# Attention output of three batches transposed by DMA instead of TensorE, with the early weight loads, the warm-up and the instruction order changed along with it

## The chip, the cores and the metric

The kernel runs on one core of a Trainium2 chip. The metric is the device time of one execution in microseconds (us). The kernel before had been measured at 306.03 us, the median of three runs from 305.15 to 315.46 us; the verdicts "faster", "same" and "slower" are set at 2%.

Engines are named as in the profile: PE is TensorE, PEld its weight loads, DVE is VectorE, ACT is ScalarE, POOL is GpSimd, and SP is SyncE, which issues most DMAs here. PSUM is the memory that matmuls write their results to. "First HP" is the first matmul of the feed-forward part, and "HP to end" is the time from its start to the end of the last matmul.

## The reference, cut to what matters

There are 4 batches with 8 heads, 768 positions and head dimension 64. Each query chooses, by a bound on its scores, 6 of 24 chunks of 32 keys, and attends causally to those. The attention output, 3072 tokens of 512 values, goes through two matrix products with a hard-swish between.

```python
ub  = sum(maximum(q * k_min, q * k_max))          # per query and chunk of 32 keys
top = argsort(where(causal, ub, -1e9))[..., -6:]
attn = softmax(where(in_top_chunk & causal, q @ k.T / 8, -1e9))
x = (attn @ v).transpose(0, 2, 1, 3).reshape(3072, 512)
h = x @ w_in                                      # w_in 512 x 2048
out = (h * clip(h + 3, 0, 6) / 6) @ w_out         # w_out 2048 x 512
```

## The kernel before

The program is planned in Python. Each operation is given to a planner with its engine, its dependencies and the ring buffers that it takes; a string `SEQUENCE` of priorities decides the order in which the planner emits ready operations. The 32 head-and-batch combinations go in 16 pairs of heads, four pairs for each batch. For a pair, K and Q are loaded and transposed on PE (tiles KT, QT), bounds and chunk choice are made (UBP, SEL, SLT), scores go to SPS, ACT takes the exponential into PT, POOL applies the causal mask, and PE multiplies by V (PVP). DVE's norm writes the attention output Xb, tokens on the partitions. The feed-forward part needs it with features on the partitions (XT). It works in eight groups of 384 tokens, two for a batch.

The attention of the next batches is interleaved with the feed-forward part of earlier ones, so that PE always has something to do. In code and in profile lines, `...` stands for what is left out.

```python
WARMUP = (10, 9)
...
    def castv():          # pair i's V, to bf16 on POOL; its operation is st[i]["o_v"]
...
    WGATE = (0, 0, 0, 4, 4, 0, 8, 3)   # weight load n is issued after the V cast of pair WGATE[n]
    ...
            iss = add("POOL", 0.63, f"w{n}",
                      lambda c=c: nc.gpsimd.dma_start(WIN[:, :, c:c + DFF // 4], wi[:, :, c:c + DFF // 4]),
                      deps=[st[WGATE[n]]["o_v"]], chain="wi")        # chain: w0, w1, ... in this order
...
        def do_xt():
            for k0 in range(0, KT_HID, 2):
                def tr(k0=k0, ps=ps):                      # 6 transposes of 128x128 on PE
                    T = new(ps, [P, 2, GRP], BF16, "XTP")
                    for kk in range(2):
                        for t in range(TPG):
                            nc.tensor.transpose(T[:, kk, t * P:(t + 1) * P],
                                                xb[b].obj[:, blk0 + t, (k0 + kk) * P:(k0 + kk + 1) * P], IDENTB[:])
                def ev(k0=k0, ps=ps):                      # and their copy out of PSUM on DVE
                    nc.vector.tensor_copy(xt.obj[:, k0:k0 + 2, :], ps.obj[:])
...
                        nc.tensor.matmul(T[:, f, 0:GRP], lhsT=WIN[:, kt, (f0 + f) * P:(f0 + f + 1) * P],
                                         rhs=xt.obj[:, kt, :], start=(kt == 0), stop=(kt == KT_HID - 1))   # HP
...
            for _ in range(WARMUP[n]):                     # before the first K, and after the first Q
                nc.tensor.transpose(T[:], IDENT32[:], IDENT32[:])
```

The softmax here doesn't subtract the row's maximum and nothing guards it: scores larger than these inputs give would overflow.

Of the kernel before, what the change touches and what calls it, by code (L numbers as in the profile page):

```python
# [15 lines left out]
P = 128  # L16
# [113 lines left out]
WARMUP = (10, 9)  # L130
# [4 lines left out]
Q10 H6.10 q15 O4.1.0 P10.0 L0 H7.4 H7.12 P10.1 U4 P5.1 R1 S10.1 V5 K0 S8.1 H7.6 R0 H3.8 H3.6 X4.2 H7.10 V10  # L135
O3.0.4 S9.0 L13 S0.3 q0 U0 P12.1 O2.1.0 H1.10 O6.0.8 U10 v0 S4.4 O6.1.8 H7.14 X1.0 X7.2 O2.0.4 K2 P4.1 K4 S11.1
L4 v12 O3.2.0 S0.1 O7.0.8 C1 W0 C7 K10 X3.2 v2 L5 k6 q2 Q2 v13 O3.0.12 v9 Q15 O2.0.8 C5 V2 O5.1.0 P6.0 P9.1
H5.12 O6.1.12 L12 O0.1.0 k1 H2.6 S5.1 v15 S0.5 H3.0 w5 Q1 H6.14 q14 B3 S0.0 O1.2.12 H1.2 U9 H7.0 k15 V4 L11 S0.4
H0.6 Q11 K6 H2.12 O1.0.4 v10 U2 O0.0.12 X7.0 C13 v3 Q14 S11.4 q10 P1.1 P9.0 O6.1.4 O3.1.8 S3.3 U3 K9 O3.1.4 B4
O4.0.12 H4.0 H6.0 S14.2 Q3 S7.0 H2.4 S7.2 O1.2.8 H1.12 K13 H1.14 B1 k2 X3.0 S10.4 K8 O6.0.12 H2.10 S13.1 w0 S9.1  # L140
H3.4 H4.4 H0.12 U1 R10 O3.2.8 O7.1.12 S3.1 P7.1 O6.0.0 S2.2 V9 O2.2.0 K3 B7 U15 P8.1 Q5 S2.1 R3 O4.0.0 H7.2
O1.0.12 H2.14 S6.1 P2.1 O4.0.4 H0.10 H0.0 X4.0 S5.0 H2.2 O5.2.0 S8.5 w7 S14.5 v8 U7 S12.0 S2.4 R5 P8.0 O2.1.12
O6.2.4 k0 k14 O1.0.8 S2.5 B9 S10.3 k10 O4.2.8 S9.3 k13 X1.2 H0.2 O7.1.8 S11.5 k3 O4.1.8 O5.0.0 P13.1 v11 O7.0.4
S3.0 H0.14 C15 O3.0.0 K15 k8 S6.2 O0.2.0 q1 R8 k9 S8.3 R11 V1 L14 q12 L2 O2.0.12 H7.8 S7.1 H0.4 U6 S10.2 O5.1.12
O0.0.0 S14.1 V13 k4 H1.8 L7 H4.10 S6.3 H3.10 O6.1.0 S4.3 w6 S9.2 S14.0 k7 H3.14 O3.1.0 q7 S7.5 S5.4 v4 H6.6
O4.2.12 K11 O4.1.4 S6.5 P1.0 S11.0 H6.12 O1.1.8 O1.2.0 H5.0 B8 O0.1.12 S6.4 K5 P3.1 H6.4 B2 k5 H4.8 H3.2 S4.2
# [19 lines left out]
def kernel(  # L166
# [541 lines left out]
```

## Time and profile before

| what | before | where it is read |
|---|---|---|
| span of the profiled run | 304.2 us | page |
| PE busy | 290.5 us (95%) | engine table of the page |
| first HP starts | 63.55 us | the trace |
| HP to end | 237.1 us | the trace |
| the 96 XTP transposes, start to start in the stream | 0.064 us each | the trace: 72 of them take 4.6 us |

The engine table of the page of the kernel before gives busy time, share of the span and instructions of each engine.

```profile
PE 290.5 (95%) x3027; PEld 182.0 (60%) x3027; DVE 168.8 (55%) x460; ACT 178.6 (59%) x219; POOL 92.0 (30%) x168
```

An average over the whole span hides that there are two stages. The windows view cuts the span; its columns are the window, its length, then the busy time and instruction count of each engine, the granted PE clock as a share of its full speed, the DMA share and GB/s.

```profile
0.00:20.00 20.00, 14.57 (x120) 11.57 (x122) 12.21 (x39) 6.15 (x9) 15.07 (x25) 0.95 1.23 200
20.00:40.00 20.00, 16.64 (x277) 11.65 (x275) 14.11 (x61) 15.11 (x18) 11.28 (x21) 0.96 1.15 209
40.00:63.55 23.55, 22.80 (x418) 16.76 (x413) 17.83 (x71) 22.02 (x27) 16.70 (x32) 1.00 1.04 197
63.55:300.80 237.25, 236.51 (x2224) 142.03 (x2221) 124.69 (x292) 134.94 (x167) 48.97 (x90) 1.00 0.30 71
```

After the first HP PE is busy 236.5 of 237.25 us, so only less PE work seems to help there. Before it, PE is idle for 9.5 us. The waits view of PE says for what (total, times, longest):

```profile
PE KT L319 <- DMA KS<-in_k_dram: 2.9, 2, 2.1
PE SLT L436 <- DVE SEL_130 L419: 2.5, 1, 2.5
PE WRM L650 <- POOL IDENT_114 masks.py:199: 1.4, 1, 1.4
PE QT L319 <- DMA QS<-in_q_dram: 1.4, 2, 0.7
```

These are loads of K and Q and one chunk choice on DVE. The DMA engines are busy all through this stage (the last two columns of the windows), and three weight loads of 512 KB each are issued in it.

### The profile page before, as it was taken

The numbers are of one execution on the slowest core, as the hardware profiler recorded it, in microseconds if no ns is written. First come the engines' busy times: TensorE is split into PE (matmuls) and PEld (weight loads), VectorE is DVE, ScalarE is ACT, GpSimd is POOL, SyncE is SP. The second block draws the span as 40 slices with busy tenths as digits, with TensorE's granted clock in tenths as the row PEclk, the third lists the DMA queues.
The fourth block names the chain that finished last, engine by engine and source line by source line (L and its number), as shares of the span: only waits on it lengthen the run. The fifth ranks groups of instructions, "written<-read, shape, count | busy, mean of one in ns | idle before, by whom it ended". The sixth has DMA issues, their size and how long they took to land.

```text
span 304.2 us, 7326 instructions
## 1 busy us (share of the span) xinstructions
PE 290.5 (95%) x3027; PEld 182.0 (60%) x3027; DVE 168.8 (55%) x460; ACT 178.6 (59%) x219; POOL 92.0 (30%) x168
## 2 busy tenths in 40 slices
PE   6977899999999999999999999999999999999995
PEld 5845567766666566756555556666656765545444
DVE  4587887756769965672444165967413575505300
ACT  1547689987466258876644555496737654624311
POOL 8576566844105235612000242450303100000000
PEclk9979999999999999999999999999999999999999
DMA  9999999995807989620200131100010000011012
GB/s 171 218 214 199 214 214 219 168 197 119 139 1 171 245 184 241 134 54 34 54 36 36 37 110 48 37 2 1 2 71 36 2 2 0 0 72 69 34 70 71
DMA packets 83122, 29.84 MB, mean 98 GB/s; under 512 B 75792, under 2 KB 80144, under 8 KB 83088
## 3 DMA queue, kind: packets, MB, share of 16 engines
q1 hardware_dynamic: 77296, 24.78, 37.1%
q0 software_dynamic: 4224, 4.19, 8.6%
q10 hardware_dynamic: 1568, 0.39, 0.7%
q8 instruction: 24, 0.39, 0.6%
q14 instruction: 10, 0.08, 0.1%
HBM read 27.26 MB, written 6.29 MB: 110 GB/s over the span
## 4 chain that ended last, share of the span: by engine, by line
PE 84%; DMA 6%; DVE 4%; ACT 2%; issue 1%; POOL 1%; SPq 1%; ACTq 0%; DVEq 0%; POOLq 0%
PE HP L564 27%; PE OP L590 26%; PE PVP L507 7%; DMA QS<-in_q_dram 6%; PE SPS L466 6%; PE SPS L471 4%; PE UBP L386 3%; PE QT L319 3%; PE KT L319 2%; PE XTP L544 2%; PE UBQ L408 2%; PE OP L611 1%; ACT PT L477 1%; DVE KM L337 1%; PE SLT L436 1%
## 5 line engine op out<-in xcount | busy, mean ns | idle before, releaser
L477 ACT ACTIVATE PT<-SPS 128x1024 bf16<-128x1024 f32 (+1 forms) x96 | 82.2, 924 | 18.1 <-PE SPS L471 15.7
L574 DVE SCALAR_TENSOR_TENSOR GT<-U,HP 128x768 bf16<-128x768 bf16 x64 | 60.7, 953 | 51.1 <-ACT U L568 36.2
L564 PE MATMUL HP<-XT,WIN 128*128 128x384 bf16 x512 | 86.8, 326 | 0.0
L590 PE MATMUL OP<-WOUT,GT 128*128 128x512 bf16 x368 | 84.1, 380 | 0.0
L568 ACT ACTIVATE U<-HP,THREE 128x768 bf16<-128x768 f32 x64 | 57.7, 901 | 39.2 <-PE HP L564 39.1
L564 PEld LDWEIGHTS <-WIN 128*128 128x128 bf16 x512 | 49.3, 98 | 32.7
L481 POOL TENSOR_SCALAR_AFFINE_SELECT PT<-PT 128x256 bf16<-128x256 bf16 x96 | 38.6, 407 | 82.0 <-ACT PT L477 81.6
L590 PEld LDWEIGHTS <-GT 128*128 128x128 bf16 x368 | 35.0, 98 | 40.2 <-issue 1.5
L596 ACT ACTIVATE OT<-OP 128x512 f32<-128x512 f32 x23 | 13.8, 598 | 42.4 <-PE OP L590 34.9
L466 PE MATMUL SPS<-RHS,LHS 64*128 64x512 bf16 (+3 forms) x256 | 34.1, 312 | 0.7 <-ACT PT L477 0.6
L471 PE MATMUL SPS<-SELT,EM 64*128 64x288 bf16 (+6 forms) x384 | 32.5, 250 | 0.0
L512 DVE RECIPROCAL RINV<-PVP 128x6 f32<-128x6 f32 x32 | 6.0, 191 | 37.7 <-PE PVP L507 37.6
L507 PEld LDWEIGHTS <-PT 128*128 128x128 bf16 x672 | 23.2, 97 | 4.1 <-issue 1.6
L471 PEld LDWEIGHTS <-EM 64*128 64x128 bf16 x384 | 18.6, 95 | 7.6 <-issue 0.5
L352 POOL CAST LHS<-KTS 128x768 bf16<-128x768 f32 x15 | 12.4, 827 | 32.8 <-ACT KTS L333 30.0
L466 PEld LDWEIGHTS <-LHS 64*128 64x128 bf16 x256 | 11.3, 95 | 11.3 <-issue 7.5
L517 DVE TENSOR_TENSOR Xb<-PVP,RINV 128x384 bf16<-128x384 f32 x32 | 17.4, 553 | 0.8
L373 POOL CAST RHS<-QTS 128x768 bf16<-128x768 f32 x16 | 15.2, 958 | 8.5 <-ACT QTS L363 8.5
L333 ACT COPY KTS<-KT 128x768 f32<-128x768 f32 x15 | 11.9, 800 | 9.5 <-PE KT L319 8.3
L319 PE MATMUL KT<-IDENT_114,KS 128*128 128x128 f32 x96 | 14.2, 292 | 2.9 <-DMA KS<-in_k_dram 2.9
L363 ACT COPY QTS<-QT 128x768 f32<-128x768 f32 x16 | 12.5, 810 | 4.2 <-PE QT L319 3.9
L319 PEld LDWEIGHTS KT<-IDENT_114,KS 128*128 128x128 f32 x96 | 11.8, 151 | 4.6 <-ACT PT L477 2.3
(113 smaller groups left out, 249.8 us busy)
## 6 DMA issues: line engine op xcount, KB each, us to landing
VS<-in_v_dram SPq DMA_DIRECT2D x32, 192.0 KB, 4.5
KS<-in_k_dram SPq DMA_DIRECT2D x31, 192.0 KB, 4.3
QS<-in_q_dram SPq DMA_DIRECT2D x31, 192.0 KB, 4.9
out_dram<-OT SPq DMA_DIRECT2D x23, 256.0 KB, 2.0
WIN<-in_moe_w_in_dram POOLq DMA_DIRECT2D x4, 512.0 KB, 9.2
WOUT<-in_moe_w_out_dram POOLq DMA_DIRECT2D x4, 512.0 KB, 9.4
out_dram<-OT SPq DMA_DIRECT2D x2, 128.0 KB, 1.7
KS<-in_k_dram ACTq DMA_DIRECT2D x1, 192.0 KB, 3.8
```

The source lines that it names most:

```text
L319: nc.tensor.transpose(T[:, j * P:(j + 1) * P], src.obj[:, j].rearrange("p e d -> p (e d)"), IDENT32[:])
L373: nc.gpsimd.tensor_copy(new(s["rhs"], [P, S], BF16, "RHS")[:], qts.obj[:])
L466: nc.tensor.matmul(T[:, e, c:c + hi - lo], lhsT=s["lhs"].obj[e * D:(e + 1) * D, j * P:(j + 1) * P], rhs=s["rhs"].obj[e * D:(e + 1) * D, lo ...
L471: nc.tensor.matmul(T[:, e, c:c + hi - lo], lhsT=EM[e * D:(e + 1) * D, h, j * P:(j + 1) * P], rhs=s["selt"].obj[e * D:(e + 1) * D, x:x + hi ...
L477: nc.scalar.activation(T[:, :, 0:w], sp.obj[:, :, 0:w], ACT.Exp, scale=scale)
L481: nc.gpsimd.affine_select(out=dv, in_=dv, pattern=[[0, 2], [1, P]], compare_op=A.is_ge, fill=0.0, base=0, channel_multiplier=-1)
L507: nc.tensor.matmul(T[:, qb, :], lhsT=t[:, e, c:c + P], rhs=fx(s["vb"])[:, e, j, :], start=(j == 0), stop=(j == qb))
L517: nc.vector.tensor_tensor(out=xb[b].obj[:, :, h * D:(h + 1) * D], in0=pv.obj[:, :, 0:D], in1=s[("ri", e)][:].to_broadcast([P, NBLK, D]), o ...
L564: nc.tensor.matmul(T[:, f, 0:GRP], lhsT=WIN[:, kt, (f0 + f) * P:(f0 + f + 1) * P], rhs=xt.obj[:, kt, :], start=(kt == 0), stop=(kt == KT_H ...
L568: nc.scalar.activation(new(u, [P, 2, GRP], BF16, "U")[:], hp.obj[:, :, 0:GRP], ACT.Relu, bias=THREE[:], scale=1.0)
L574: nc.vector.scalar_tensor_tensor(out=gt.obj[:, f0:f0 + 2, :], in0=u.obj[:], scalar=6.0, in1=hp.obj[:, :, 0:GRP], op0=A.min, op1=A.mult)
L590: nc.tensor.matmul(T[:, :], lhsT=gt.obj[:, f, t * P:(t + 1) * P], rhs=WOUT[:, f, :], start=(f == 0), stop=(f == FT - 1))
```

## The change

The intent has three parts. For batches 1 to 3 the DMA engines transpose Xb into XT, which takes 72 of 96 transposes from PE. Two of the three early weight loads go behind the third V cast, out of the way of the K and Q loads. The warm-up of PE's clock uses real fp32 matmuls instead of transposes. A new `SEQUENCE` (order) was found for it.

```diff
-WARMUP = (10, 9)
+WARMUP = ((6, 0.43), (8, 0.21), (3, 0.21))
...   (SEQUENCE replaced as a whole)
-    plan = Plan(rings, dict(PE=2.0, DVE=3.2, ACT=2.2, POOL=9.3, LD=0.3, ST=0.0), place)
+    plan = Plan(rings, dict(PE=1.4, DVE=3.2, ACT=2.2, POOL=9.3, LD=0.3, ST=0.0), place)
-    WGATE = (0, 0, 0, 4, 4, 0, 8, 3)
+    WGATE = (0, 2, 1, 5, 6, 5, 6, 2)
...
+            if b >= XDMA:                                   # XDMA = 1
+                for t in range(TPG):                        # TPG = 3 blocks of 128 tokens
+                    def tr(t=t):
+                        if t == 0:
+                            new(xt, [P, TPG, KT_HID, P], BF16, "XT")
+                        nc.sync.dma_start_transpose(xt.obj[:, t], xb[b].obj[:, blk0 + t, :])
+                    ops.append(add("LD", 0.7, f"X{g}.{t}", tr, deps=norms[b] + ops[:1], take=[xt] if t == 0 else [],
+                                   use=[xb[b]] if t == 0 else [xb[b], xt]))
+                return ops
...   (batch 0: as before, into the new layout of XT)
-                                         rhs=xt.obj[:, kt, :], start=(kt == 0), stop=(kt == KT_HID - 1))
+                                         rhs=xt.obj[:, :, kt, :], start=(kt == 0), stop=(kt == KT_HID - 1))
...
-            for _ in range(WARMUP[n]):
-                nc.tensor.transpose(T[:], IDENT32[:], IDENT32[:])
+            for _ in range(WARMUP[n][0]):
+                nc.tensor.matmul(T[:], lhsT=IDENT32[:], rhs=IDENT32[:], start=True, stop=True)
...
+            if i == 0 and f is plan_K:
+                plan_warm(2, st[0]['o_ktr'])                # three more, between the first K and the first Q
```

More of the change, by code (lines that the diff above doesn't have):

```diff
@@ L127, in run @@
         return order
-WARMUP = (10, 9)
+WARMUP = ((6, 0.43), (8, 0.21), (3, 0.21))
 SEQUENCE = """
-Q10 H6.10 q15 O4.1.0 P10.0 L0 H7.4 H7.12 P10.1 U4 P5.1 R1 S10.1 V5 K0 S8.1 H7.6 R0 H3.8 H3.6 X4.2 H7.10 V10
-O3.0.4 S9.0 L13 S0.3 q0 U0 P12.1 O2.1.0 H1.10 O6.0.8 U10 v0 S4.4 O6.1.8 H7.14 X1.0 X7.2 O2.0.4 K2 P4.1 K4 S11.1
-L4 v12 O3.2.0 S0.1 O7.0.8 C1 W0 C7 K10 X3.2 v2 L5 k6 q2 Q2 v13 O3.0.12 v9 Q15 O2.0.8 C5 V2 O5.1.0 P6.0 P9.1
-H5.12 O6.1.12 L12 O0.1.0 k1 H2.6 S5.1 v15 S0.5 H3.0 w5 Q1 H6.14 q14 B3 S0.0 O1.2.12 H1.2 U9 H7.0 k15 V4 L11 S0.4
@@ L139 @@
-H0.6 Q11 K6 H2.12 O1.0.4 v10 U2 O0.0.12 X7.0 C13 v3 Q14 S11.4 q10 P1.1 P9.0 O6.1.4 O3.1.8 S3.3 U3 K9 O3.1.4 B4
-O4.0.12 H4.0 H6.0 S14.2 Q3 S7.0 H2.4 S7.2 O1.2.8 H1.12 K13 H1.14 B1 k2 X3.0 S10.4 K8 O6.0.12 H2.10 S13.1 w0 S9.1
-H3.4 H4.4 H0.12 U1 R10 O3.2.8 O7.1.12 S3.1 P7.1 O6.0.0 S2.2 V9 O2.2.0 K3 B7 U15 P8.1 Q5 S2.1 R3 O4.0.0 H7.2
-O1.0.12 H2.14 S6.1 P2.1 O4.0.4 H0.10 H0.0 X4.0 S5.0 H2.2 O5.2.0 S8.5 w7 S14.5 v8 U7 S12.0 S2.4 R5 P8.0 O2.1.12
-O6.2.4 k0 k14 O1.0.8 S2.5 B9 S10.3 k10 O4.2.8 S9.3 k13 X1.2 H0.2 O7.1.8 S11.5 k3 O4.1.8 O5.0.0 P13.1 v11 O7.0.4
@@ L144 @@
-S3.0 H0.14 C15 O3.0.0 K15 k8 S6.2 O0.2.0 q1 R8 k9 S8.3 R11 V1 L14 q12 L2 O2.0.12 H7.8 S7.1 H0.4 U6 S10.2 O5.1.12
-O0.0.0 S14.1 V13 k4 H1.8 L7 H4.10 S6.3 H3.10 O6.1.0 S4.3 w6 S9.2 S14.0 k7 H3.14 O3.1.0 q7 S7.5 S5.4 v4 H6.6
-O4.2.12 K11 O4.1.4 S6.5 P1.0 S11.0 H6.12 O1.1.8 O1.2.0 H5.0 B8 O0.1.12 S6.4 K5 P3.1 H6.4 B2 k5 H4.8 H3.2 S4.2
-q13 O0.1.4 B13 V3 O1.1.12 v6 Q12 Q8 H4.6 C8 B12 H1.6 H6.2 B6 S4.1 O3.2.12 v7 P11.0 S4.5 B10 O4.1.12 S7.4 O0.0.4
-H1.4 P0.1 S8.4 O2.1.8 P15.1 H4.12 X2.2 S2.0 S7.3 k11 w4 O7.0.12 S1.4 B11 H5.14 L3 S8.0 w1 U5 H3.12 q5 V15 v14
@@ L149 @@
-C14 O2.2.12 v5 B14 S4.0 S12.1 S8.2 C2 S13.0 X5.2 S3.5 S12.3 P14.0 R12 S1.3 O4.2.4 O2.1.4 O5.0.8 O0.1.8 S9.5 S3.2
-B15 S5.3 q6 C9 R4 S6.0 O5.0.4 O7.2.0 P2.0 S1.1 P11.1 S5.5 S15.5 X2.0 q9 S14.3 C0 V7 P6.1 H2.0 O2.0.0 q8 L1 H4.2
-q4 H0.8 Q6 O7.1.4 H4.14 S9.4 K1 L15 O3.0.8 q11 U13 S3.4 O2.2.8 O4.0.8 V12 S13.2 S5.2 H5.2 S15.3 P7.0 U11 O7.2.12
-P13.0 V14 C6 H2.8 P0.0 S10.5 U12 w3 P4.0 U14 O3.1.12 H1.0 H5.10 S11.3 R7 V8 q3 S12.2 Q4 V11 O1.2.4 W1 R2 O5.1.4
-H6.8 O0.2.8 O5.1.8 P14.1 C11 L9 C10 S15.1 S15.4 O7.1.0 O6.2.12 K7 C3 V0 S10.0 S0.2 O6.2.0 C12 L6 v1 C4 K12 w2
@@ L154 @@
-K14 B5 S13.5 S12.5 O7.2.8 H5.6 O0.0.8 O2.2.4 P12.0 R9 O4.2.0 S13.3 O6.2.8 O5.2.4 X5.0 Q13 L8 V6 O0.2.12 O6.0.4
-R15 O3.2.4 U8 P5.0 O0.2.4 X0.0 R14 S15.2 S14.4 L10 Q7 P15.0 X6.2 O5.2.12 S12.4 B0 S13.4 O5.0.12 S1.5 Q9 R13 X6.0
-O5.2.8 Q0 S1.2 S11.2 O7.0.0 O1.1.0 k12 H5.4 H5.8 S15.0 R6 S2.3 S1.0 P3.0 X0.2 O1.1.4 O1.0.0
+H6.10 H7.14 Q10 H7.12 H7.4 P5.1 H3.6 P10.1 q15 P12.1 K9 S8.1 O6.1.8 v12 X7.2 O3.0.12 v0 H3.8 H6.14 q10 X3.2
+S10.1 S11.1 K4 O3.0.4 R0 U4 L13 P10.0 U10 S9.0 P4.1 S6.4 S0.3 q14 L11 H6.0 Q15 O6.1.4 P9.1 Q5 O6.1.12 q0 v2
@@ new lines @@
+O3.2.0 S0.0 q2 P9.0 k10 H2.12 Q11 S5.1 V5 H7.0 S7.0 L0 X1.0 H2.14 V9 P8.0 K8 k14 H7.10 v9 H3.0 X2.1 H0.10 H3.4
+v10 K0 q1 U3 S4.4 S13.1 R8 X3.1 R5 C7 H2.4 O1.2.12 C1 S0.5 S6.3 H2.10 O2.0.4 v13 K13 k1 K10 H6.12 B1 O6.0.12 R1
+O4.1.0 O6.0.8 P6.0 H3.10 H1.14 X6.1 O7.0.8 O6.2.4 w5 H7.6 S12.0 V4 O6.0.0 O1.0.12 H0.14 O3.2.8 V10 B7 k9 Q14
+O2.1.0 O4.2.8 H2.6 S9.3 R10 S8.5 P8.1 H0.6 S0.1 S2.1 L5 U0 H1.10 B3 S12.1 O1.0.8 K6 V2 U15 O3.1.4 C0 H1.12 K11
+L4 P11.0 S0.4 S9.1 H0.0 k15 H4.0 O4.0.0 U2 Q2 P13.1 H0.2 w0 V12 H1.2 B4 U9 O0.0.12 H0.4 v3 O5.1.0 W0 S8.2 S10.2
@@ new lines @@
+Q8 X4.2 H0.12 H6.6 B9 O5.0.0 B15 k6 S2.2 L12 R3 P1.1 w6 X4.1 O1.1.12 O5.2.0 S7.2 k3 H6.4 W2 O4.0.12 q12 O4.1.12
+q13 X3.0 S8.3 H3.12 L2 S11.4 v11 Q3 V1 S10.4 U5 O3.1.8 S14.5 O1.0.4 S6.2 L14 q7 C5 O7.1.12 k8 U8 k11 O4.1.8
+O3.1.12 S14.0 O2.0.12 q8 S3.3 S6.0 Q12 Q1 S2.4 C13 P13.0 P7.0 S9.4 K1 H6.2 O1.2.4 v8 O1.1.8 V15 P15.1 O1.2.0 R12
+H5.12 O5.1.12 H7.2 S5.0 v15 O2.0.8 O0.1.4 H2.2 X2.2 X1.2 X7.0 O7.1.8 k0 H2.0 R11 S11.0 S7.1 O7.2.12 B5 w7 H3.14
+S1.3 S8.4 H7.8 X7.1 S14.3 S4.3 H4.8 S4.1 O4.0.4 S2.5 U6 B8 X5.2 S15.5 O2.2.0 k13 v6 S5.3 S7.5 q6 S8.0 S9.2 K15
@@ new lines @@
+v4 H1.8 H5.2 k2 q4 P0.1 U7 S5.4 v5 P7.1 O4.2.12 S6.5 v7 O3.1.0 O0.1.0 q5 P3.1 O1.2.8 O5.0.8 H0.8 S4.5 S7.4 S1.4
+L7 V3 S3.1 O3.0.8 S1.1 V7 O0.1.12 S7.3 k7 B13 H5.10 S2.0 S3.0 P1.0 S11.5 U13 P11.1 O6.2.8 W1 V8 O4.2.4 P4.0 V13
+S4.0 V11 O7.0.4 Q6 H2.8 B10 C15 k5 S13.0 X2.0 O0.0.0 U1 O2.2.8 U12 P6.1 O3.2.12 L8 L6 U14 O6.2.12 P14.0 S10.3 Q4
+S5.5 S9.5 P2.0 K2 C8 w4 w3 O6.1.0 X6.2 V6 S14.1 O0.1.8 k4 S14.2 S10.0 R13 S6.1 U11 B12 P2.1 S5.2 O4.1.4 O3.0.0
+S13.2 O2.1.8 P12.0 X5.1 C14 K12 O2.2.12 O2.1.12 L15 H1.6 H6.8 H3.2 L1 H5.0 K3 H4.4 V0 q11 H4.6 O2.1.4 v14 C6 L9
@@ new lines @@
+H4.10 O7.1.4 B6 S15.3 H4.2 C3 O6.2.0 S4.2 O7.2.0 H1.0 C10 O0.2.0 O7.1.0 X4.0 S0.2 C11 C2 B2 S11.3 O5.1.4 O4.0.8
+w1 H5.14 S13.5 O6.0.4 P5.0 S10.5 S15.1 P14.1 O7.2.8 L3 K14 P0.0 H4.12 O5.1.8 R7 S12.4 S3.5 O2.0.0 S12.5 S12.3 R4
+O0.0.4 K5 C9 S11.2 C12 O7.0.12 O4.2.0 S15.4 Q13 R9 R2 S12.2 O0.2.12 V14 O1.1.0 O3.2.4 S1.2 q3 X6.0 H4.14 R14 L10
+B14 S3.2 R15 S3.4 B0 H1.4 X5.0 R6 q9 C4 Q0 S14.4 B11 w2 X0.0 v1 k12 H5.8 S1.5 H5.6 O1.1.4 O0.0.8 K7 P15.0 O0.2.4
+O5.0.4 O5.2.4 S15.2 O5.2.8 S13.3 O1.0.0 S13.4 O0.2.8 S1.0 S15.0 O5.2.12 O2.2.4 O7.0.0 O5.0.12 Q9 H5.4 Q7 P3.0
@@ L157 @@
+S2.3 X0.2
 """
@@ L327, in plan_K @@
         tr = add("PE", 0.66, tok, lambda: transposed(kt, s["ks"], "KT"), deps=[s["ldk"]], take=[kt], use=[s["ks"]], chain="K")
+        s["o_ktr"] = tr
         direct = i == 0
@@ L527 @@
     last_o = [None]
+    XDMA = 1
     def plan_mlp(g, wdma):
@@ L548, in ev @@
                     if k0 == 0:
-                        new(xt, [P, KT_HID, GRP], BF16, "XT")
-                    nc.vector.tensor_copy(xt.obj[:, k0:k0 + 2, :], ps.obj[:])
+                        new(xt, [P, TPG, KT_HID, P], BF16, "XT")
+                    nc.vector.tensor_copy(xt.obj[:, :, k0:k0 + 2, :].rearrange("p t k s -> p k t s"),
+                                          ps.obj[:].rearrange("p k (t s) -> p k t s", s=P))
                 tok = f"X{g}.{k0}"
@@ L563, in mm @@
                     for kt in range(KT_HID):
-                        nc.tensor.matmul(T[:, f, 0:GRP], lhsT=WIN[:, kt, (f0 + f) * P:(f0 + f + 1) * P],
-                                         rhs=xt.obj[:, kt, :], start=(kt == 0), stop=(kt == KT_HID - 1))
+                        nc.tensor.matmul(T[:, f, 0:GRP].rearrange("p (t s) -> p t s", s=P), lhsT=WIN[:, kt, (f0 + f) * P:(f0 + f + 1) * P],
+                                         rhs=xt.obj[:, :, kt, :], start=(kt == 0), stop=(kt == KT_HID - 1))
             def relu():
@@ L648, in mm @@
             T = new(w, [P, P], FP32, "WRM")
-            for _ in range(WARMUP[n]):
-                nc.tensor.transpose(T[:], IDENT32[:], IDENT32[:])
-        return add("PE", 0.2 * WARMUP[n], f"W{n}", mm, deps=[after], take=[w], chain="warm")
+            for _ in range(WARMUP[n][0]):
+                nc.tensor.matmul(T[:], lhsT=IDENT32[:], rhs=IDENT32[:], start=True, stop=True)
+        return add("PE", WARMUP[n][1] * WARMUP[n][0], f"W{n}", mm, deps=[after], take=[w], chain="warm")
     for i in range(NP):
```

## The prediction

> **What bounds it now.** TensorE. The page's engine table has PE busy 290.5 of 304.2 us, ACT 178.6, DVE 168.8. Windows split this: up to the first HP matmul at 63.7 us PE is busy 54.2 (9.5 idle); from there to 300.8 us it is busy 236.4 of 237.1; the last 3.4 us are the final eviction and store. So after 63.7 us only less TensorE work helps. Before it, starts and waits count: the waits view gives 2.9 us for KS loads, 2.5 for SEL_130 (DVE), 1.4 for QS loads. The chain of waits holds one QS load of 13.6 us (19.9 to 33.5), issued just after three 512 KB WIN loads (17.6 to 22.2 us) joined a DMA at 218 GB/s. The granted clock is 0.50 from 18 to 21 us, after PE idled about 2.5 us; estimate: 1.8 us of array time lost.
>
> **What the change removes.** 72 of 96 XTP transposes. In the chain twelve take 0.78 us, six 0.33 to 0.36, so 0.06 each: 4.3 us of a full TensorE. Their 12 DVE copies (0.55 us) are off the path. Warm-up W1 (9 fp32 transposes, 1.9 us in the chain) becomes 8 fp32 matmuls, plus 3 where PE waits for QS: about even. The instruction orders, weighted with these durations, hold 4.7 us less TensorE work; the work ahead of the first HP is the same (46.5 against 46.8).
>
> **What it moves.** Two of the three early WIN loads go behind the third V cast (36.8 us before), so the K/Q loads meet 2 MB of reads less (9 us at 218 GB/s). I expect the 13.6 us QS wait to shrink to about 5, the KS wait of 2.1 at 29 us to vanish, and HP to start near 58 instead of 63.7; then ACT (92% busy from 40 to 60 us) and DVE limit it. "TensorE: Matmul & The Clock Gate", Part 4, in the Trainium skill says that transposes do not count as busy to the clock gate as matmuls do. Here six fp32 KT transposes take 1.54 us at 4.6 us and 0.82 at 13.4, so transposes alone did warm it, only late. Matmuls should warm it before 8 us: about 1 us, within the 5.7. The half clock at 18 us may stay, since the SEL wait ahead of it stays.
>
> **What it adds.** 18 DMA transposes of 128x512 bf16 (128 KB), SP queue, in order. "DMA: Bandwidth & Descriptors", "Latency and other measured facts", gives 261 GB/s for a non-contiguous DMA transpose; estimate 0.5 us each, plus about 2 us to land as the 256 KB stores here show, plus 0.4 to 0.8 us issue on SP. The orders leave 7 to 9 us of other TensorE work between a batch's last PVP and its first HP. Norm 1.5, four issues about 3 and landing 2 fit, barely. I allow 2 us of stalls in three batches. The strided rhs of HP should stream unchanged (0.1625 us per matmul).
>
> **Sum.** 306.0 - 4.3 - 5.7 + 2 = 298.0 us. Range 293 to 304. Faster by over 2%: 0.62; within: 0.31; slower: 0.07.
>
> **Checks.** Busy PE down about 4 to 6 us; XTP count 24; first HP at 56 to 60 us; HP spacing unchanged; waits of PE for XT DMAs under 3 us in total; DMA transposes landing in under 3.5 us; the tail unchanged.
>
> **What would break it.** Slow or serialized DMA transposes (over 3 us each would put 3 to 10 us of stall on each of three batches), or SP blocked: a V load waiting for its buffer stands between two transposes of batch 1. Weights arriving late for batch 0's HP or OP. An ACT bound before 60 us that keeps HP near 62: then about 302.

## The result, and the profile after

The changed kernel took 301.79 us (median of four runs, 301.43 to 302.06). The kernel before took 308.17 us in the four runs beside it (305.15, 306.03, 310.32 and 315.46). The ratio of fast runs is 0.9875, with a 95% interval of 0.9844 to 0.9905, a gain of 1.25%. A ratio here is the mean time of one kernel's fast runs over that of the other's fast runs of the same rounds, so it is not quite the ratio of the medians quoted. Here 0.9875 is what the four runs against 305.15 and 306.03 alone give; 310.32 and 315.46 are over 1.5% above the fastest, so they count as slow. Set 2 shows what such a 310 is.

The forecast was 298.0 us, a gain of 2.6%. The time fell inside the range, but the gain was less than half of what was forecast.

The engine table, the windows (now cut at the new first HP) and PE's waits of the kernel after:

```profile
PE 287.3 (96%) x2948; PEld 178.4 (59%) x2970; DVE 163.6 (55%) x448; ACT 178.3 (59%) x219; POOL 92.5 (31%) x168
```

```profile
0.00:20.00 20.00, 16.25 (x149) 12.87 (x151) 11.90 (x42) 8.06 (x11) 14.72 (x25) 0.91 1.18 191
20.00:40.00 20.00, 19.29 (x309) 13.62 (x306) 16.67 (x75) 15.55 (x21) 13.61 (x25) 0.92 1.13 205
40.00:60.52 20.52, 19.97 (x375) 14.67 (x374) 15.17 (x54) 18.82 (x24) 13.28 (x26) 1.00 1.06 209
60.52:296.50 235.98, 231.79 (x2124) 137.28 (x2143) 119.91 (x280) 135.58 (x167) 50.89 (x93) 1.00 0.37 84
```

```profile
PE SPS L468 <- ACT PT L479: 1.3, 4, 0.6
PE HP L578 <- DMA XT<-Xb: 1.0, 1, 1.0
PE SLT L438 <- DVE SEL_130 L421: 0.9, 1, 0.9
PE QT L320 <- DMA QS<-in_q_dram: 0.8, 1, 0.8
...
PE KT L320 <- DMA KS<-in_k_dram: 0.3, 1, 0.3
```

The first HP starts 3.0 us earlier (60.52 against 63.55), and the waits for K loads are nearly gone. After it, PE is no longer busy all the time: 231.8 of 236.0 us by these records (22 of 2143 matmul records, all of OP, are missing in this trace, so the idle time is an upper bound; the time from first HP to end doesn't depend on it). 2143 is the 2221 matmuls of before, less the 72 transposes and six score matmuls (SPS) that the new order puts ahead of the first HP. Six such matmuls take 0.46 us at 124.36 us in the kernel before. HP to end went from 237.1 to 235.8 us. Taking out 4.6 us of transposes there gave 1.3 us in this profile; 3.3 us came back in another form.

Some of it came back at the DMA transposes. Part 6 of the page says that one lands 2.5 us after its issue (median), which was expected. The timeline of SP ahead of batch 3's first HP, and of PE at the same place (start, duration, engine and line, operation, count, and in brackets the idle time before it and its releaser):

```profile
244.62 5.15 SPq L546 DMA_TRANSPOSE XT<-Xb  x4
249.87 0.53 SPq L613 DMA_DIRECT2D out_dram<-OT  x1
250.44 2.53 SPq L546 DMA_TRANSPOSE XT<-Xb  x2
```

```profile
243.05 7.08 PE L604 MATMUL OP<-WOUT,GT 128*128 128x512 bf16 x31 [0.22 <-DVE Xb L519]
251.15 1.46 PE L578 MATMUL HP<-XT,WIN 128*128 128x384 bf16 x8 [1.01 <-DMA XT<-Xb]
```

SP needs about 1.3 us for each of these issues (5.15 for four). The first HP of group 6 needs three transposes, but four were issued in the first stretch, because one of group 7, which is needed much later, stands second in the order. The third that group 6 needs was issued fourth, at about 248.5 us, and PE waited 1.01 us for it. At the first HP of each of the three batches the distance from the matmul before was 0.50, 0.49 and 1.39 us (at 130.5, 187.7 and 249.8 us) where 0.216 us is normal: together 1.7 us. The rest of the 3.3 us was in many small gaps; the experiments look for their cause.

### The profile page after: what moved, and what is told of

Read it like the earlier page. It is cut to its first block, busy times and chain, and to the rows that moved or that the text cites. A ratio compares the mean times of both kernels' runs of the same rounds, so it can differ in the third digit from the quotient of the medians.

```text
span 300.2 us, 7214 instructions
## 1 busy us (share of the span) xinstructions
PE 287.3 (96%) x2948; PEld 178.4 (59%) x2970; DVE 163.6 (55%) x448; ACT 178.3 (59%) x219; POOL 92.5 (31%) x168
## 4 chain that ended last, share of the span: by engine, by line
PE 82%; DVE 4%; ACT 4%; DMA 3%; SPq 2%; issue 2%; POOL 1%; ACTq 0%; DVEq 0%; POOLq 0%
PE HP L578 28%; PE OP L604 22%; PE PVP L509 8%; PE SPS L468 7%; PE SPS L473 5%; PE UBP L388 4%; PE QT L320 3%; PE KT L320 3%; ACT PT L479 2%; PE UBQ L410 2%; SPq L546 2%; DMA XT<-Xb 2%; DMA KS<-in_k_dram 1%; PE OP L625 1%; PE SLT L438 1%
## 5 line engine op out<-in xcount | busy, mean ns | idle before, releaser
L604 PE MATMUL OP<-WOUT,GT 128*128 128x512 bf16 x346 | 82.6, 379 | 1.6 <-issue 0.3
L339 DVE TENSOR_REDUCE KM<-KTS 128x24 f32<-128x768 f32 x15 | 13.9, 943 | 4.4 <-ACT KTS L335 4.3
L320 PE MATMUL KT<-IDENT_114,KS 128*128 128x128 f32 x96 | 13.5, 284 | 0.5 <-DMA KS<-in_k_dram 0.3
```

Of the source, the lines that this page charges most:

```text
L320: nc.tensor.transpose(T[:, j * P:(j + 1) * P], src.obj[:, j].rearrange("p e d -> p (e d)"), IDENT32[:])
L604: nc.tensor.matmul(T[:, :], lhsT=gt.obj[:, f, t * P:(t + 1) * P], rhs=WOUT[:, f, :], start=(f == 0), stop=(f == FT - 1))
```

## The experiments

In each experiment but those named a repeat, only what its text names is changed and the order of instructions on every engine is held fixed: the emission order was recorded from the kernel named and is replayed, so the planner can't move anything else. 18 kernels were run in five sets; each had its own runs of the kernel before on the same chip. "Ratio" is always against those. First HP and HP to end come from the profiled execution.

How far one profile can be trusted shows where several have the same order. HP to end is 237.14 us in all three with TensorE transposes in the old order (before, before_again, b_wg). With the order of the changed kernel it is 235.8, 236.1, 236.4, 236.5 and 236.6 us (the changed kernel, after_again, a_w0late, a_wgold, a_warmold; mean 236.3). The first profile was thus at the low end, and the gain there is 0.9 us in the mean rather than 1.3. The first HP with the changed start is at 60.52, 59.83, 60.29 and 60.03 us (the changed kernel, after_again, a_xfirst, a_nox). A difference of less than about 0.8 us between two single profiles says little.

### Set 1: one part of the change undone or moved, in the new order

**a_xfirst.** The three DMA transposes of the group that is needed first are issued first.

```diff
 SP order:  - X6.0 X7.0 X6.1 X6.2 ...
            + X6.0 X6.1 X6.2 X7.0 ...          (and so for groups 2 and 4)
```

> The changed kernel, every engine's order held, but the three DMA transposes of a batch's first group are issued back to back on SP, before the second group's and before V loads and stores. Theory S (part of the expected gain went into HP waiting for the third transposed block: start-to-start gaps of 1.39, 0.50 and 0.49 us at the first HP of batches 3, 1 and 2 where 0.22 is normal, 1.7 us in all): 1.2 to 1.7 us faster than the change's 301.8, so 300.1 to 300.6, and no wait of PE for XT is left. Rival R (these waits only show where another one would come, so removing them moves the wait): within 0.5 us of 301.8, another wait in their place.

Measured: 299.90 us (299.21 to 300.27), ratio 0.9703 [0.9652, 0.9754]. First HP 60.29, HP to end 234.4, and no wait of PE for XT is left in its waits view. The order of the issues cost the changed kernel about 1.9 us of its time (301.79 to 299.90), and 1.4 us of HP to end, or 1.9 against the mean of 236.3. (a_warmold, with the old order of issues in the same set, took 301.67.)

**a_xpe.** The transposes of batches 1 to 3 go back to PE, and all else stays as changed.

```diff
-    XDMA = 1
+    XDMA = 4
```

> The changed kernel, orders held, but batches 1 to 3 are transposed by TensorE again (72 transposes and 12 DVE copies put in where the buffers allow). Theory P (TensorE is full after the first HP: 4.6 us of work come back, 1.7 us of waits for XT go): 2.4 to 3.4 us slower than the change, 304.2 to 305.2. Rival Q (the transposes sat in slack, so taking them away gained nothing and the whole gain is from the start of the kernel): within 0.7 us of 301.8. First HP stays at 60.5 us in both.

Measured: 307.05 us (306.69 to 309.43), ratio 0.9949 [0.9893, 1.0005]. It is 5.3 us slower than the changed kernel: the direction is right, the size is more than expected. Its profile, of its slowest execution (309.43), has the first HP at 61.9 where 60.5 was expected, HP to end 242.3, and gaps of up to 0.9 us from start to start before XTP blocks (at 249.7 us): they were put at the first places that the buffers allowed, and not tuned. So its size is no clean price of the transposes.

**a_wgold.** The weight loads are issued where they were before.

```diff
-    WGATE = (0, 2, 1, 5, 6, 5, 6, 2)
+    WGATE = (0, 0, 0, 4, 4, 0, 8, 3)
```

> The changed kernel, orders held, but the weight loads are issued where the kernel before had them (three at the first V cast). Theory L (the early gain is the K and Q loads that no longer queue behind 2 MB of weights): first HP 2 to 3 us later than 60.5, time 303.5 to 305. Rival W (it is the warm-up or the new order): first HP within 0.7 us, time within 0.7 us of 301.8.

Measured: 312.70 us (312.08 to 313.67), ratio 1.0118 [1.006, 1.0176], so 11 us slower than the changed kernel and slower than the kernel before. The first HP was at 71.62. PE waited 7.3 us for one K load:

```profile
PE KT L379 <- DMA KS<-in_k_dram: 7.7, 2, 7.3
```

Undone in the new order, the weight gates thus cost more than any other part; that isn't their worth on their own (b_wg below). The size was far off what had been expected, and set 2 shows why.

**a_warmold.** The warm-up is that of before (10 and 9 transposes).

```diff
-                nc.tensor.matmul(T[:], lhsT=IDENT32[:], rhs=IDENT32[:], start=True, stop=True)
+                nc.tensor.transpose(T[:], IDENT32[:], IDENT32[:])
```

> The changed kernel, orders held, but the old warm-up: 10 and 9 fp32 transposes, none between the first K and Q. Theory W (the warm-up gives 1 us or more of the early gain): first HP 1 to 2 us later, time 302.8 to 303.8; QT of the first pair takes about 1.5 us instead of 0.82. Rival L (loads and ACT bound the start, the warm-up moves only work that waits anyway): time within 0.5 us of 301.8.

Measured: 301.67 us (301.32 to 303.36), ratio 0.9772 [0.9719, 0.9825], first HP at 60.00. The new warm-up was worth nothing, to about 0.5 us. It does work as intended: the first Q's transposes took 0.82 us in the kernel after and 1.52 in a_warmold. But the next wait, for a Q load at about 13.8 us, ends at nearly the same time in both.

```profile
6.73 0.82 PE L320 MATMUL QT<-IDENT_114,QS 128*128 128x128 f32 x6
...
13.77 0.41 PE L320 MATMUL QT<-IDENT_114,QS 128*128 128x128 f32 x2 [0.76 <-DMA QS<-in_q_dram]
```

```profile
6.68 1.52 PE L379 MATMUL QT<-IDENT,QS 128*128 128x128 f32 x6 [0.36 <-DMA QS<-in_q_dram]
...
9.33 0.82 PE L379 MATMUL KT<-IDENT,KS 128*128 128x128 f32 x6
...
13.91 0.30 PE L379 MATMUL QT<-IDENT,QS 128*128 128x128 f32 x1 [0.75 <-DMA QS<-in_q_dram]
```

The first fence is of the kernel after, the second of a_warmold.

### Set 2: the kernel before once more, and the two causes together

**before_again.** The kernel before, unchanged, profiled again. The runs of set 1 had shown the kernel before at about 305.8 us in some executions and about 310 us in others.

> The kernel before itself, unchanged, to see what its two groups of times are (305.1 to 306.0 and 309.5 to 310.3 us). Theory L (in the longer group the fifth pair's K load lands later, so TensorE waits for it much longer than the 2.1 us of the first profile, as the 7.3 us of the run with the early weight loads): if the profile falls in the group near 310, its wait of the fifth KT for KS is 5 to 8 us, and its first HP is at 67 to 69 us instead of 63.5, with the rest unchanged. Rival C (the half-clock windows make the two groups): the KS wait is about 2 us in both and the lost time is spread over matmuls of half speed.

Measured: 309.42 us median, with single times of 305.45, 307.12, 309.21, 309.63, 309.84 and 309.85. Over all rounds, the 60 runs of the kernel before under 311 us are 22 from 305.1 to 306.2 us (mean 305.6), 35 from 308.7 to 310.5 us (mean 309.7) and three between. The profile that the prediction was made from was of the lower group, this one is of the upper (span 308.1). HP to end is 237.1 us in both; the first HP is at 67.45 in the upper one. Here are the POOL, SP and PE timelines where the two part, before first and before_again second:

```profile
17.64 1.63 POOL L302 DMA_DIRECT2D WIN<-in_moe_w_in_dram  x2
...
21.40 0.76 POOL L302 DMA_DIRECT2D WIN<-in_moe_w_in_dram  x1
...
17.29 1.67 SPq L272 DMA_DIRECT2D KS<-in_k_dram  x2
...
29.30 0.85 PE L319 MATMUL KT<-IDENT_114,KS 128*128 128x128 f32 x6 [2.14 <-DMA KS<-in_k_dram]
```

```profile
17.29 1.80 POOL L302 DMA_DIRECT2D WIN<-in_moe_w_in_dram  x2
...
19.62 0.76 POOL L302 DMA_DIRECT2D WIN<-in_moe_w_in_dram  x1
...
17.62 2.75 SPq L272 DMA_DIRECT2D KS<-in_k_dram  x2
...
32.02 1.51 PE L319 MATMUL KT<-IDENT,KS 128*128 128x128 f32 x6 [6.74 <-DMA KS<-in_k_dram]
```

The two K loads of the fifth pair and the first two weight loads are issued within 0.35 us of each other. In the lower group K goes first, in the upper group the weights do (here the third weight load comes 1.8 us sooner as well), and PE waits 6.74 us for K instead of 2.14. The chain of waits of before_again has a K load of 13.43 us (from 18.46 us) on it. After so long an idle time PE also runs slowly: the same six transposes take 1.51 us instead of 0.85. The granted clock in the trace is 0.5 for 6.8 us from 29.2 us, 3.9 us into that wait, which agrees with the Trainium skill ("TensorE: Matmul & The Clock Gate", Part 1, "What's actually happening"), by which the clock halves after an idle window of about 3.4 us. (It is not the whole rule: the first profile has half clock for 3.4 us from 18.0 us, after a wait of 2.5 us only.)

Against the mean of the lower group (305.6) the changed kernel's gain is 3.8 us, against that of the upper (309.7) it is 7.9 us. The changed kernel has one group. The four later profiles with the old weight gates (a_wgold, b_nox, b_none, b_none1) also have the weights first, by 0.30 to 1.25 us, and PE waits 5.9 to 7.3 us for that K; in b_none1 the third weight load comes as late as in the lower group. So six profiles agree, but only one of them has K first. That the early weight loads make the upper group is tested by b_wg below; the order of issue was never changed alone, and what decides it wasn't looked for.

**a_w0late.** The first weight load, too, goes behind the third V cast.

```diff
-    WGATE = (0, 2, 1, 5, 6, 5, 6, 2)
+    WGATE = (2, 2, 1, 5, 6, 5, 6, 2)
```

> The changed kernel, orders held, but the first WIN load too is issued only at the third V cast, so no weights stand ahead of the fifth pair's K and Q loads. Theory L (the start is still bound by loads: the fifth KT waited 1.4 to 1.9 us for KS in three of the four profiles of the changed orders): that wait goes, first HP at 57.5 to 59 us, time 299.5 to 301. Rival A (from the first exp on, ACT, DVE and TensorE together set the pace, so HP starts at 60 whatever the loads do): first HP 59.7 to 60.5, time within 0.6 us of 301.8.

Measured: 301.45 us (300.29 to 302.37), ratio 0.9797 [0.9741, 0.9853]; first HP at 59.63, only 0.9 us earlier (and 0.2 us earlier than in after_again), although the first PVP starts 1.8 us earlier (25.83 instead of 27.59). So by now something other than the loads sets the start.

**a_both.** a_w0late with a_xfirst.

> Both edits together: the first WIN load late and the three DMA transposes of a batch's first group issued first. If the two costs are separate, the gains add: 1.9 us for the transposes as measured, and 1 to 2 us (theory L) or 0 to 0.6 us (rival A) for the weights: 298 to 299 under L, 299.3 to 300.2 under A.

Measured: 299.24 us (298.93 to 302.64, and one slow run of 306.33), ratio 0.9742 [0.9671, 0.9813]; first HP 59.35, HP to end 234.1. The two don't add up to more than a_xfirst alone, within the spread. The two high times, and one of 302.88 us in m_one below, were not explained.

**b_all.** All of the change except its new order: DMA transposes, weight gates and warm-up put into the recorded order of the kernel before.

> All of the change except its new order: the order of the kernel before on every engine, with the DMA transposes where the TensorE transposes stood, the new weight gates and the new warm-up. Theory S (the new order is what hides the DMA transposes, three issues of about 1.26 us and 2.5 us to land, 5 to 6 us in all; the old order leaves 3 to 6 us between the last normalised head and the first HP): waits of PE for XT of 6 to 10 us in total, first HP near 60.5, time 304 to 309. Rival N (the new order matters only for the start): waits for XT under 3 us, time within 1 us of 301.8.

Measured: 312.44 us (310.15 to 314.57), ratio 1.0156 [1.0089, 1.0222], slower than expected. PE waited for XT at the start of every batch:

```profile
PE HP L637 <- DMA XT<-Xb: 6.5, 3, 2.3
```

HP to end was 244.1. The DMA transposes need an order in which other PE work stands between a batch's last PVP and its first HP, and most of the new order's worth is there. In the order of before, HP follows too soon after PVP for that.

### Set 3: the weight gates alone, and what paces the start

**b_wg.** The kernel before with the new weight gates, and nothing else but the new layout of XT.

```diff
-    WGATE = (0, 0, 0, 4, 4, 0, 8, 3)
+    WGATE = (0, 2, 1, 5, 6, 5, 6, 2)
```

> The kernel before with only the weight loads moved to the new gates: order, TensorE transposes and warm-up of before. Theory L (two of the change's parts count: late weights for the start, DMA transposes with the new order for the rest): the KS wait of 2 to 7 us is under 2 us, first HP near 60.5, time 302 to 304 in one group of times, not two. Rival O (the new order is needed for the early gain too): two groups remain, or first HP over 62.5, time 305 or more.

Measured: 305.44 us (304.58 to 306.48), ratio 0.995 [0.989, 1.0009]; first HP 62.82, HP to end 237.1. All six times lie in one group, beside a kernel before that showed both (305.35 to 309.95 on the same chip). So the early weight loads were what made the upper group, and the new gates take that group away. Against the lower group they gain next to nothing. One reason is in the waits: PE waits for K only 1.3 us in all, but now 1.8 us for a mask on POOL at 34 us, because POOL issues two weight loads (1.51 us, from 33.83 us) ahead of that mask. The rest of the early gain needed the new order: b_all, with the new warm-up as well, has its first HP at 62.93.

**p_act, p_pe, p_dve.** What paces the 59 us before the first HP in a_both? Work is added to one engine at a time, in pairs 2 to 6: ten extra ACT copies of 0.81 us (8.1 us in all), sixty extra fp32 transposes on PE (6.6 us), or ten extra chunk reductions on DVE of 0.93 us (9.3 us).

```diff
 p_act: +                if 2 <= i <= 6:
        +                    nc.scalar.copy(kts.obj[:], kt.obj[:, 0:S])            (and so for QTS)
 p_pe:  -        for j in range(NBLK):
        +        for j in list(range(NBLK)) * (2 if twice else 1):                 (KT and QT)
 p_dve: +            for _ in range(2 if 2 <= i <= 6 else 1):
                         stat(A.max, s["KM"][:])                                   (and so for A.min)
```

> The version with both edits (299.0 us, first HP at 59.4), every PSUM copy on ACT of pairs 2 to 6 done twice: 10 more ACTIVATE COPY of 0.81 us, 8.1 us more ACT work ahead of the first HP, same result. Theory A1 (ACT alone sets the pace ahead of HP): HP later by 6 to 8 us. Theory A3 (ACT, DVE and TensorE wait for each other in turn, none alone): later by 3 to 5 us. Theory L (loads set it): under 2 us.

> The same version, the KT and QT transposes of pairs 2 to 6 done twice: 60 more fp32 transposes of 0.11 us, 6.6 us more TensorE work ahead of the first HP, same result. A1: HP later by under 2 us. A3: by 2.5 to 5 us. L: under 2 us.

> The same version, both chunk reductions of pairs 2 to 6 done twice: 10 more TENSOR_REDUCE of 0.93 us, 9.3 us more DVE work ahead of the first HP, same result. A1: HP later by under 2 us. A3: by 3 to 6 us. L: under 2 us.

| run | added | time, us (range) | ratio | first HP, us | first HP later, of the added work |
|---|---|---|---|---|---|
| a_both | - | 299.24 | 0.9742 | 59.35 | - |
| p_act | 8.1 us ACT | 304.14 (302.94 to 304.34) | 0.9898 | 63.33 | 4.0 us, 0.49 |
| p_pe | 6.6 us PE | 303.17 (303.08 to 303.81) | 0.988 | 63.89 | 4.5 us, 0.69 |
| p_dve | 9.3 us DVE | 307.41 (306.70 to 308.33) | 1.0014 | 68.22 | 8.9 us, 0.95 |

DVE's work comes through almost in full, PE's to two thirds and ACT's to a half. The start is a chain through all three, and work added to DVE shows most; the prediction had named ACT and DVE. POOL and the DMA rate were not tested. The p_dve profile has half clock for 6.8 us from 19.0 us and the other three have none, so part of its 8.9 us may be a slower PE. That part looks small: the changed kernel has 6.8 us of half clock too, and its first HP is only 0.2 and 0.5 us later than in a_xfirst and a_nox, which have none. Before the first HP, PE is busy 55.5 us in the changed kernel and 52.8 in a_xfirst, and idle 5.0 and 7.5: what the slow clock took would else have been waiting. a_both ran in the set before, on another chip, so these are comparisons of profiles between sets.

### Set 4: what is left when nothing waits for XT, and fewer DMA transposes

**a_nox.** A wrong result: in the changed kernel, HP of batches 1 to 3 reads a constant tile, so it never waits for XT. The DMA transposes are still issued.

```diff
-                                         rhs=xt.obj[:, :, kt, :], start=...
+                                         rhs=(XT0 if b >= XDMA else xt.obj)[:, :, kt, :], start=...
```

> The changed kernel, orders held, the 18 DMA transposes still issued, but HP of batches 1 to 3 reads a constant tile instead (result wrong on purpose), so no matmul waits for a transpose. Theory E (the new order has about 1.6 us of waits of its own after the first HP): from the first HP to the last matmul 234.1 us, time near 300.1. Rival D (the DMA transposes cost the rest too, by holding SP or the DMA engines): 232.5 us, time near 298.5.

Measured: 299.95 us (299.63 to 300.19), ratio 0.9784 [0.9703, 0.9864]; HP to end 234.6. That is what a_xfirst has (299.90 and 234.4) with a correct result. So the waits for XT were worth 1.2 us of HP to end (1.7 against the mean of 236.3; 1.8 us of time), and something else holds the gain of 4.6 us down to 2.5.

**b_nox.** Wrong too: the same constant tile in the order, gates and warm-up of the kernel before. If the new order brought waits of its own, this should reach 232.5 us from first HP to end.

> The same constant tile in the old order with old weight gates and warm-up, DMA transposes issued in place of the TensorE transposes (result wrong on purpose). Theory E: the old order without the 4.6 us of transposes takes 237.1 - 4.6 = 232.5 us from the first HP to the last matmul. Rival D: 233.5 us or more. First HP as in the kernel before, 63.5 or 67.5 us by its two groups.

Measured: 305.95 us (303.62 to 308.48, both groups again), ratio 0.9958 [0.9854, 1.0062]; HP to end 234.6, the same as a_nox. The blame on the new order falls. In the old order, too, taking out 4.6 us of transposes frees 2.5. The waits view after the first HP shows what came in their place. First the kernel before, then b_nox:

```profile
PE UBP L386 <- DVE QP L367: 0.5, 1, 0.5
```

```profile
PE SPS L529 <- ACT PT L540: 1.6, 5, 0.4
PE HP L639 <- ACT PT L540: 0.4, 1, 0.4
PE SLT L499 <- DVE SEL L482: 0.2, 1, 0.2
```

PE waits 2.2 us there, almost all for ACT's exponentials. Three of the waits stand just ahead of the first HP of batch 1:

```profile
127.53 0.39 PE L529 MATMUL SPS<-RHS,LHS 64*128 64x512 bf16 x2 [0.38 <-ACT PT L540]
...
128.44 0.39 PE L529 MATMUL SPS<-RHS,LHS 64*128 64x512 bf16 x2 [0.39 <-ACT PT L540]
...
129.36 0.39 PE L529 MATMUL SPS<-RHS,LHS 64*128 64x256 bf16 x4 [0.33 <-ACT PT L540]
```

They are 0.91 us apart, about the time of one exponential on ACT (0.94 us: six take 5.61 us in the timelines below). In the kernel before the same place looks so:

```profile
123.58 0.84 PE L544 MATMUL XTP<-IDENTB,Xb 128*128 128x128 bf16 x12
124.36 0.39 PE L466 MATMUL SPS<-RHS,LHS 64*128 64x512 bf16 x2
124.59 0.30 PE L471 MATMUL SPS<-SELT,EM 64*128 64x288 bf16 x4
124.82 0.88 PE L544 MATMUL XTP<-IDENTB,Xb 128*128 128x128 bf16 x12
```

And ACT's timeline has the same run of six exponentials without a gap in both, first before, then b_nox:

```profile
122.95 5.61 ACT L477 ACTIVATE PT<-SPS 128x1024 bf16<-128x1024 f32 x6 [0.72 <-PE SPS L471]
```

```profile
126.45 5.61 ACT L540 ACTIVATE PT<-SPS 128x1024 bf16<-128x1024 f32 x6 [0.72 <-PE SPS L534]
```

The new theory is that the transposes stood where ACT set the pace, and cost nothing there. Set 5 tests it.

**m_one.** One DMA transpose of 128x1536 for a group, in place of three of 128x512, on a_both.

```diff
-                for t in range(TPG): ... dma_start_transpose(xt.obj[:, t], xb[b].obj[:, blk0 + t, :])
+                dma_start_transpose(T[:].rearrange("p t k s -> p (t k) s"),
+                                    xb[b].obj[:, blk0:blk0 + TPG, :].rearrange("p t d -> p (t d)"))
```

> The version with both edits, but one DMA transpose of 128x1536 per group in place of three of 128x512. Theory B (issue time goes with the blocks of 128 columns: 1.26 us for 4, so 3.8 us for 12): landing and time as with three, 298.8 to 299.5. Rival I (issue time is mostly per DMA): lands 2 us sooner; as no wait for XT is left, time still within 0.5 us of 299.1.

Measured: 298.60 us (298.20 to 299.53, and one slow run of 302.88), ratio 0.9745 [0.9685, 0.9805]; first HP 58.99, HP to end 234.2. The XT lines of the tile view, of the changed kernel and then of m_one (shortest, median and longest issue in ns, first and last start), and the time to landing:

```profile
L546 SPq DMA_TRANSPOSE XT<-Xb x18: 1196/1262/2145, 122.4 to 251.7; - x18
...
DMA to landing us min/median/max: 2.4/2.5/4.7
```

```profile
L605 SPq DMA_TRANSPOSE XT<-Xb x6: 1430/1652/2542, 121.0 to 244.2; - x6
...
DMA to landing us min/median/max: 3.9/4.1/5.1
```

The issue costs SP 1.65 us for a whole group, where three took 3.8 (3 x 1.26): it is mostly a cost of each DMA and not of its bytes. The group's data are there 4.1 us after the start of the issue; with three it is 2 x 1.26 + 2.5 = 5.0 us. That saves 0.9 us of latency, but the order already covers it, and the time isn't separated from a_both's: its ratio to the kernel before is 0.9745 against 0.9742. Both beat the kernel before and the changed kernel.

**after_again.** The changed kernel once more, beside these.

> The changed kernel itself, unchanged, again. One group of times, 301.4 to 302.1 us as before; against the kernel before a ratio between 0.976 (if its runs fall near 310) and 0.9875 (near 305.5), so the verdict depends on the group that the kernel before falls in.

Measured: 301.72 us (300.93 to 303.12), ratio 0.9851 [0.9794, 0.9908]; HP to end 236.1. The first result is confirmed. m_one is 3.1 us faster on the same chip.

### Set 5: are removed transposes free where ACT sets the pace?

**b_none.** As b_nox, and no DMA transpose is issued at all (wrong). If the DMA transposes or the SP queue took the 2.1 us, they come back now.

```diff
-                        nc.sync.dma_start_transpose(xt.obj[:, t], xb[b].obj[:, blk0 + t, :])
+                        pass
```

> Wrong result on purpose: as b_nox (order, weight gates and warm-up of the kernel before; HP of batches 1 to 3 reads a constant tile), and now no DMA transpose is issued at all. In b_nox TensorE waited 2.2 us after the first HP, 1.6 of it for ACT's exponentials (SPS<-ACT PT), where the kernel before waited 0.5. Theory ACT pace: the transposes that were taken out had stood in stretches where ACT's exponentials set the pace, so TensorE now waits there; the DMA transposes have nothing to do with it. Then first HP to the end of the last matmul stays 234.6 (234.1 to 235.1), with SPS waits on ACT of 1.2 to 2.2 us after the first HP. Rival D: the DMA transposes or the SP queue are what TensorE lost the 2.1 us to; then 232.5 to 233.3 and the waits on ACT fall under 0.7.

Measured: HP to end 235.15, not less than b_nox's 234.6; 307.38 us (303.28 to 307.97), ratio 0.9933 [0.9813, 1.0053]. Its waits for ACT after the first HP are the same:

```profile
PE SPS L529 <- ACT PT L540: 1.6, 5, 0.4
```

So no cost of the DMA transposes to PE beyond the waits for XT shows here. (The profiled execution is of the upper group, with a K wait of 7.2 us start to start. From first HP to end its granted clock is full, so this part may be compared; the total times of b_nox, b_none and b_none1 mix both groups and are not used.)

**b_none1.** As b_none, and batch 1's 24 transposes stand on PE again, where the kernel before has them, with their copies on DVE.

```diff
-    XDMA = 1
+    XDMA = 2                        (the order of batch 1 is that of before)
```

> Wrong result on purpose: as b_none, but the 24 TensorE transposes (and their four copies on DVE) of batch 1 stand again where the kernel before has them. They take 1.6 us of TensorE (24 of 0.065). Theory ACT pace: they stand between score matmuls that wait for ACT at 127 to 130 us in b_nox (1.1 us in three waits), so most of them is free: first HP to the end is at most 0.7 us more than in b_none, and the three waits for ACT before batch 1's first HP are gone or under 0.3. Rival: TensorE's own work is what counts there, and it is 1.3 to 1.7 us more.

Measured: HP to end 234.77. Without those 24 transposes (1.6 us of PE work) it was 235.15 in b_none, which has one more wait of 0.5 us for DVE, and 234.59 in b_nox. So they cost between -0.4 and 0.2 us, which is nothing within the spread of the profiles. The time is 307.97 us (306.17 to 308.76), ratio 0.9989 [0.9899, 1.0078]. The three waits at batch 1 are gone:

```profile
PE SPS L529 <- ACT PT L540: 0.5, 2, 0.3
```

So a third of the removed work had been free, within about 0.5 us: where it was taken out, PE waits for ACT instead. That accounts for about 1.6 of the 2.1 us of gain missing in the old order. For batches 2 and 3 it is only read from the waits (0.3, 0.2 and 0.4 us for ACT and DVE at 204 to 239 us in b_nox), not tested. In the new order a_nox still has 1.7 us without PE work after the first HP (232.8 of 234.6 busy, no record missing), although six score matmuls have moved ahead of it; its longest waits there are one of 0.6 us for ACT and one of 0.4 us that the profile gives no cause for, the others are of 0.2 us. What each of them hangs on wasn't tested and stays open.

## Why the prediction was wrong

Two steps failed. The early gain was the larger miss: 5.7 us forecast, 3.0 measured. The other was the step from a busy PE to a gain: 4.3 us of transposes were taken as 4.3 us of time, and about 2.5 were there to be had. The allowance for stalls was right, and the base was one of two levels of the kernel before. The forecast sum was 306.0 - 4.3 - 5.7 + 2 = 298.0; the two profiles give 306.0 - 3.0 - 1.3 + 0.3 (a longer tail) = 302.0, against 301.9 in the profiled execution.

| step of the prediction | forecast | measured |
|---|---|---|
| HP starts earlier (loads, warm-up) | 5.7 us, to 58 | 3.0 us, to 60.5 |
| of it, the warm-up | about 1 us | under 0.5 us (a_warmold) |
| transposes removed | 4.3 us gained | 4.6 us removed, about 2.5 gained without any XT wait (b_nox; a_nox the same) |
| stalls for XT | 2 us | 1.7 us of gaps in the trace (1.0 in the waits view); 1.9 us of time (a_xfirst) |
| HP spacing unchanged | yes | yes, 162 ns start to start in both |
| DMA transposes land in | under 3.5 us | 2.5 us |
| busy PE down | 4 to 6 us | 3.2 us (290.5 to 287.3, with records missing after); 3.4 in after_again (287.1, none missing) |
| XTP count; last matmul to end of span | 24; unchanged | 24; 3.55 us before, 3.85 after |

1. **"4.3 us of a full TensorE."** Here the mechanism failed. It took PE's busy share of 236.5 of 237.25 us as proof that any removed PE work is gained. A full PE can be full of work that fits into another engine's pace: in the kernel before, batch 1's transposes stood between score matmuls that would have waited for ACT, and ACT ran its six exponentials in 5.61 us with or without them. b_none1 shows that 24 of the 72 were free. For the other 48, and for the new order, the cause of what is missing stays open.
2. **The early gain of 5.7 us.** The mechanism was right and its size was not. The waits view of the kernel before has only 4.3 us of waits for K and Q loads; 3.2 of them went (1.1 are left), and none of those left is after 14 us. With the first weight load late too (a_w0late, a_both, m_one), HP still doesn't start before 59.0 us, as work added to DVE, PE or ACT delays it (p_dve, p_pe, p_act). The prediction said that "ACT (92% busy from 40 to 60 us) and DVE limit it" then, and warned of "An ACT bound before 60 us that keeps HP near 62". So it named two of the three that limit the start, and set that limit 2.5 us too early.
3. **The 2 us of stalls.** This was right, for the reason given, that SP's issues run in order. What it missed is that a block of the second group stands among the three that the first group needs. SP's issue was 1.26 us each, against the forecast's 0.4 to 0.8, so putting the three first gains 1.9 us (a_xfirst).
4. **The warm-up.** The prediction cited the Trainium skill ("TensorE: Matmul & The Clock Gate", Part 4), by which transposes do not count as busy for the clock gate as matmuls do. Here the real matmuls raised the rate about 2.6 us sooner (0.82 us for six transposes at 6.7 us instead of at 9.3), but transposes alone reached it too, and the gain was lost in the next wait for Q.
5. **The base of 306.0.** Nothing in three runs and one profile showed that the kernel before has two groups of times, about 4 us apart. The chosen profile was of the lower one. The weight gates, whose effect the prediction expected in the first HP of that profile, mostly act by removing the upper group (b_wg). Against the upper group, the gain is 7.9 us; that the forecast against the lower was 8.0 is chance.

The DMA estimate of the prediction (0.5 us for 128 KB at the 261 GB/s of "DMA: Bandwidth & Descriptors", section "Latency and other measured facts", plus 2 us to land) gives the measured 2.5 us, but partly by chance: the 2.5 us count from the start of an issue of 1.26 us, which the prediction put at 0.4 to 0.8 us and added. No run separates the rate from the fixed part for certain. From 128 KB to 384 KB the landing grows by 1.6 us (2.5 to 4.1), which as an estimate is 0.8 us for each further 128 KB, part of it the longer issue.

## What to carry to other kernels

Before you count work taken off a full engine as gain, look at what stands on both sides of it: if the neighbours belong to a chain that another engine paces, as score matmuls behind exponentials do here, the work was filling a gap, and its removal uncovers a wait. When a load is issued within a few tenths of a microsecond of a large one on another queue, one profile may show only one of two outcomes; look at the spread of many runs for two groups, and gate the large one. Issue in-order transfers in the order of their first use, and merge small ones: here a DMA transpose took 1.26 us of its queue to issue, and one three times as large only 1.65.

## What the Trainium skill lacked or had wrong

- "DMA: Bandwidth & Descriptors" gives a rate for DMA transposes and their constraints. It has no time in us for what the issue costs on SP at these sizes, and none from issue to landing for a small one from SBUF to SBUF. Measured: issue 1.26 us and landing 2.5 us for 128x512 bf16, issue 1.65 us and landing 4.1 us for 128x1536. The order of issues decided 1.9 us of 301.8.
- "VectorE: DVE Perf Modes", section "The three transpose paths", sets 390 ns on TensorE against 1309 ns by DMA for 128x128 bf16. In a stream of transposes TensorE needed 64 ns for each (start to start), and one DMA moved four such blocks in 2.5 us. The table has one figure for each path; the rate in a stream, and the issue and landing of a DMA that holds several blocks, are not in it.
- "TensorE: Matmul & The Clock Gate", Part 4, says that the full clock doesn't engage for transposes (its times there are for bf16). Here fp32 transposes alone brought the shorter time: six of them went from 1.54 us (at 4.8 us) to 0.82 us (at 9.3 us) in a_warmold. Part 1's idle window of about 3.4 us ("What's actually happening") agrees with the half clock of 6.8 us that began 3.9 us into a wait of 6.74 us, but that window alone doesn't account for the rest: half clock for 3.4 us also followed a wait of 2.5 us (before, at 18.0 us), and the changed kernel had 6.8 us of it from 16.4 us with no wait over 1 us there.
- None of the pages that this case drew on names two levels of run time that go with which of two nearly simultaneous DMA issues is first: 305.6 and 309.7 us for the same kernel, and one level (304.6 to 306.5) with two of the weight loads gated later.
